# One chain of softmax sums for both query halves, part of a sum on TensorE, and copies and stores handed to other engines

## The chip, the cores and the metric

The kernel runs on one core of one Trainium2 chip. The metric is the device time of one execution in microseconds (us); a lower value is better. The profile shows one execution on that core: the start and duration of the instructions of every engine, and the DMA traffic. The engines are named as the profile names them: PE is TensorE (matmuls; PEld is its weight load), DVE is VectorE, ACT is ScalarE, POOL is GpSimd, and SP is SyncE, which here only starts DMAs.

## The reference

Two blocks follow each other. The first is an attention in which a key counts only if it falls into the same hash bucket as the query; the second mixes with a two-dimensional Fourier transform and then runs a two-layer network with a normalization ahead of it. Cut to what matters:

```
q, k, v: (4, 8, 768, 64)     proj: (64, 6)     w_ch1: (512, 2048)     w_ch2: (2048, 512)

q_bucket = sum(((q @ proj) > 0) * 2**arange(6));  k_bucket likewise
scores = where(q_bucket[:, None] == k_bucket[None, :], q @ k.T / 8, -1e9)
attn   = exp(scores - max);  attn /= sum(attn) + 1e-9
x      = attn @ v                        # then (B,H,S,D) -> (B, S, H*D) = (4, 768, 512)

u  = x + real(fft(fft(x, axis=seq), axis=channel))
un = (u - mean(u)) / sqrt(var(u) + 1e-6)
out = u + relu(un @ w_ch1) @ w_ch2
```

## The kernel before

The four batches are four rounds. In each round attention works on pairs of heads: NPAIR = 4 pairs a batch, two heads of 64 channels side by side on the 128 partitions. For one pair n the 768 keys are taken in NT = 6 chunks of 128 keys (index c), and the 768 queries in two halves of 384 (index g).

**One chunk.** `weigh(n, c)` makes the scores on PE (L849 adds the bucket bits as a bf16 product for the first five pairs, L856 is q times k), and ACT writes their exponential to one of two buffers `pk` (L860). For the later pairs DVE masks it (L866). DVE then adds the chunk to a running sum `acc` (L939): for chunk 1 it adds chunks 0 and 1, for every later chunk it adds the chunk to `acc`. For the first batch it does so in two instructions of 128x768, for the later batches in one of 128x1536. `values(n, c, ...)` multiplies the weights with v on PE (L877); it is put one chunk later in the program, behind the scores of the next chunk, and so the values of a pair's last chunk come behind the scores of chunk 0 of the next pair.

**The end of a pair.** After the values of chunk 5, `scale(n, oos, acc)` normalizes the pair. It copies a column `vs` out of PSUM (L886, on DVE), ACT adds `vs` to both halves of the result while it moves them to `x` (L889), and then each half g is treated alone: two PE matmuls with a matrix of ones sum `acc` over the 128 keys, one for each head, into the upper and lower 64 partitions of one PSUM bank (L894); DVE transposes that bank in blocks of 32x32 into `rt` (L900), takes every 32nd column (12 of them), adds a small number (L902), takes the reciprocal (L903), copies each of the 12 values to 32 places (L905, the spread copy), transposes back into `rb` (L909) and multiplies `x` by it (L910).

**The second block.** `fold` (L989 to L1007) makes sums and differences of `x` on DVE. `mix(b)` then multiplies with the channel matrix on PE (L1029) into a PSUM bank `cs`, from which ACT copies the forward half into `F` (L1036) and DVE the half that runs backward (L1042). A second product (L1058) gives two banks A and B for each of four groups of channels, and four DVE instructions add them to `x` (L1074), two for each bank. The two-layer network follows (`mlp0` for the first batch, `mlp7` for the others; L1296, L1343, and `outer7` with L1214 and L1226). It is written with fewer and larger products in the manner of Strassen, and ends with the stores of `out` by `store` (L967), which POOL issues. A batch has 16 stores.

**The order of the work.** `ps_1` has two PSUM banks for everything that is not scores or values. The first batch's attention runs together with `weights1`, which brings w_ch1 from 64-bit floats to 32 bits: each of its 16 slices costs DVE three instructions (L631, L635, L641) and ACT three (L639, L646, L647). After four slices, and again after eight, `average` computes column means on PE (L654) and `centre` takes them off on DVE (L662, four instructions). This part, from the start to about 131 us, stands in `tc.manual_schedule`[...]. After it, each round runs attention(b) and mix(b-1) with its network side by side, and a planner that works with its own costs and priorities sets the order of each engine's instructions. The last round is mix(3) alone.

At the end every engine leaves through a conditional branch (L1477, L1495: a flag says whether a slower version for very large scores must run), and SP and POOL close the program (L1526).

Of the kernel before, what the change touches and what calls it, by code (L numbers as in the profile page):

```python
# [11 lines left out]
F32 = mybir.dt.float32  # L12
# [5 lines left out]
ALU = mybir.AluOpType  # L18
AX = mybir.AxisListType

P = 128
B, H, S, D = 4, 8, 768, 64
# [3 lines left out]
NT = S // P  # L26
NPAIR = H // 2
HALF = S // 2
# [18 lines left out]
EPS = 2.0**-90  # L47
# [432 lines left out]
def _main(  # L480
# [13 lines left out]
    nc = tc.nc  # L494
# [13 lines left out]
    def wt(shape, dtype, tag, name, bufs=2):  # L508
        return work.tile(shape, dtype, tag=tag, name=name, bufs=bufs)
# [4 lines left out]
    def pt(shape, name):  # L514

        turn[0] += 1
        if roomy[0] and turn[0] % 2:
            if turn[0] % 4 == 1:
                return ps_o.tile(shape, F32, tag="o", name=name)
            return ps_sc.tile(shape, F32, tag="sc", name=name)  # L520
        return ps_1.tile(shape, F32, tag="ps", name=name)
# [72 lines left out]
    ones = const.tile([P, D], F32, tag="ones", name="ones")  # L594
# [8 lines left out]
    for i in range(NPK):  # L603
        pk = const.tile([P, 2, 2, HALF + 1], F32, tag=f"pk{i}", name=f"pk{i}")
# [226 lines left out]
    @contextmanager  # L831
    def behind():

        with tc.issue_after(last[0].ins), tc.high_priority(offset=AHEAD):
            yield
# [43 lines left out]
                    pk[:, g, h, 0:w], start=(c == 0), stop=(c == NT - 1),  # L879
                )  # L880

    def scale(n, oos, acc):

        x = xs[n // NPAIR][:, n % NPAIR]
        vs = wt([P, 1], F32, "vs", f"vs{n}")
        nc.vector.tensor_copy(vs, oos[0][:, HALF : HALF + 1])  # L886
        halves = [x[:, g * HALF : (g + 1) * HALF] for g in range(2)]
        for g, xg in enumerate(halves):
            nc.scalar.activation(xg, oos[g][:, 0:HALF], AF.Identity, bias=vs)  # L889
        for g, xg in enumerate(halves):  # L890

            ps = pt([P, HALF], f"sum{n}_{g}")
            for h in range(2):
                nc.tensor.matmul(  # L894
                    ps[h * D : (h + 1) * D, :], ones, acc[:, g, h],
                    start=True, stop=True,
                )

            rt = wt([P, HALF], F32, "rt", f"rt{n}_{g}", 1)
            nc.vector.transpose(rt, ps)  # L900
            rc = wt([P, HALF // 32], F32, "rc", f"rc{n}_{g}")
            nc.vector.tensor_scalar(rc, rt[:, 0:HALF:32], S * EPS, None, op0=ALU.add)  # L902
            nc.vector.reciprocal(rc, rc)  # L903
            rb = wt([P, HALF], F32, "rb", f"rb{n}_{g}", 1)
            nc.vector.tensor_copy(  # L905
                rt.rearrange("p (j i) -> p j i", i=32),
                rc[:, :, None].broadcast_to([P, HALF // 32, 32]),
            )
            nc.vector.transpose(rb, rt)  # L909
            nc.vector.tensor_tensor(xg, xg, rb, op=ALU.mult)  # L910

    def attention(b):
        xs[b] = wt([P, NPAIR, S], F32, "x", f"x{b}")
        pending = []

        def finish():
            n, c, pk, oos, acc = pending.pop(0)
            with behind() if n >= NPAIR and t is not None else nullcontext():
                values(n, c, pk, oos)
            if c == NT - 1:  # L920
                scale(n, oos, acc)

        for t in range(NPAIR):
            n = NPAIR * b + t
            half = fold(b, 0) if t == NPAIR - 1 else iter(())
            if 1 < n + 1 < NPAIR * B:
                load(n + 1)
            ahead = prepare(n + 1) if n + 1 < NPAIR * B else iter(())
            oos = [ps_o.tile([P, 512], F32, tag="o", name=f"oo{n}_{g}") for g in range(2)]
            acc = wt([P, 2, 2, HALF], F32, "t6", f"acc{n}", 2)  # L930
            first = None
            for c in range(NT):
                new = weigh(n, c)
                if c == 0:
                    first = new[:, :, :, 0:HALF]
                else:

                    for g in (0, 1) if b == 0 else (slice(0, 2),):
                        nc.vector.tensor_tensor(  # L939
                            acc[:, g], (first if c == 1 else acc)[:, g],  # L940
                            new[:, g, :, 0:HALF], op=ALU.add,
                        )
                while pending:
                    finish()
                pending.append((n, c, new, oos, acc))
                if c > 2:
                    next(half, None)
                if c > 0:
                    next(ahead, None)
                yield  # L950
        t = None
        while pending:
            finish()
# [5 lines left out]
    def store(b, T, src, cols):  # L959

        blk, r = divmod(T * P, HALF)
        at = 0
        while at < P:
            par, i = divmod(r + at, HW)
            w = min(P - at, HW - i)
            s0 = blk * HALF + 2 * i + par
            nc.gpsimd.dma_start(  # L967
                out[b, s0 : s0 + 2 * w - 1 : 2, cols], src[at : at + w, cols]
            )
            at += w  # L970
# [41 lines left out]
    def mix(b):  # L1012
        x = xs[b]
        yield from fold(b, 1)
        z = zs[b]


        hd = DM // 2
        F = wt([P, 2, 2, 2, DM], F32, "F", f"F{b}", 1)
        nc.gpsimd.memset(F[:, :, 1, :, 0 : hd + 1 : hd], 0.0)  # L1020
        for par in range(2):
            for t in range(NT // 2):
                ps = pt([P, DM], f"cs{b}_{par}_{t}")
                kinds = (0, 1) if t == 1 else (par ^ (t // 2),)
                for pc in range(2):
                    lo = 0 if 0 in kinds else hd // 2 + 1 - pc
                    hi = hd if 1 in kinds else hd // 2 + 1 - pc
                    for cp in range(2):
                        nc.tensor.matmul(  # L1029
                            ps[:, pc + 2 * lo : pc + 2 * hi - 1 : 2],  # L1030
                            z[:, cp, pc, par, t * P : (t + 1) * P],
                            ch[:, cp, pc, lo:hi], start=(cp == 0), stop=(cp == 1),
                        )
                f = F[:, par, :, t % 2]
                for k in kinds:
                    nc.scalar.copy(  # L1036
                        f[:, k, k : hd + 1 - k],
                        ps[:, k * (hd + 1) : DM if k else hd + 1],
                    )
                f = f[:, kinds[0] : kinds[-1] + 1, hd + 1 :]  # L1040
                r = ps[:, (kinds[0] + 1) * hd - 1 : (kinds[0] + 1) * hd]
                nc.vector.tensor_copy(  # L1042
                    f,
                    bass.AP(
                        r.tensor, r.offset, [r.ap[0], [hd, len(kinds)], [-1, hd - 1]]
                    ),
                )
                yield

        for j in range(NDC):
            pa, pb = (pt([P, HALF + 1], f"{nm}{b}_{j}") for nm in "AB")
            for par in range(2):
                cols = slice(par * NK, HALF + 1 if par else NK)
                for k, ps in enumerate((pa, pb)):
                    for t in range(2):
                        nc.tensor.matmul(  # L1058
                            ps[:, cols], F[:, par, k, t, j * P : (j + 1) * P],
                            sq[:, t, k, cols], start=(t == 0), stop=(t == 1),  # L1060
                        )

            for i in range(2):
                u = x[:, j, i * HALF : (i + 1) * HALF].rearrange("p (r n) -> p r n", r=2)
                for ps, op in (
                    (pa, ALU.add), (pb, ALU.subtract if (j < 2) ^ i else ALU.add)
                ):
                    if i == 0:
                        f = ps[:, 0 : 2 * NK - 1]
                        f = bass.AP(f.tensor, f.offset, [f.ap[0], [NK, 2], [1, HW]])  # L1070
                    else:
                        f = ps[:, HW : HALF + 1]
                        f = bass.AP(f.tensor, f.offset, [f.ap[0], [HW, 2], [-1, HW]])
                    nc.vector.tensor_tensor(u, u, f, op=op)  # L1074
            yield

        yield from mlp0(b) if b == 0 else mlp7(b)
# [111 lines left out]
    def outer7(b, half, hall, ut, rs):  # L1189
# [14 lines left out]
        for j in range(GT):  # L1204
# [35 lines left out]
            if half:  # L1240
                store(b, j, u, low)
# [196 lines left out]
    for b in range(B):  # L1438
# [17 lines left out]
        if b == B - 1:  # L1456
# [7 lines left out]
            ps = pt([1, 3, P], "norms_t")  # L1464
# [13 lines left out]
        for _ in other:  # L1478
            pass
        other = mix(b)  # L1480
        if b == 0:
            arrival2 = weights2()
# [48 lines left out]
```

## Time and profile before

| what | value |
|---|---|
| time, median of 3 runs | 1128.34 us (1127.03 to 1129.04) |
| the profiled execution: its time, and the span of its profile | 1127.22 us, 1125.4 us |
| PE busy | 1067.8 us, 95% of the span |
| DVE busy | 813.7 us, 72% |
| ACT busy | 445.8 us, 40% |
| POOL busy | 81.3 us, 7% |
| last DVE instruction ends | 1115.67 us after the start |
| stores of `out` | 64, of which 16 belong to the last batch |

"Busy" is the time in which an engine has at least one instruction running. A share over the whole span mixes stages: the first batch's attention with the conversion of w_ch1 (up to about 150 us) loads DVE far more than the rest, and after about 200 us PE is busy nearly all the time. A number in a group of instructions such as "x128 | 25.5, 494" is the count, the busy time in us, and the mean duration of one in ns; PE overlaps its instructions, so that the count times the mean exceeds the busy time. PE takes a product of 32-bit floats as two records, so 128 records at L894 are 64 matmuls.

### The profile page before, as it was taken

To read this page: it belongs to the slowest core of one execution; us is meant where nothing else is said; L and a number is where in the kernel's file an instruction comes from. 1 tells how busy PE (TensorE), PEld (TensorE's weight loads), DVE (VectorE), ACT (ScalarE), POOL (GpSimd) and SP (SyncE) were. 2 spreads that over 40 slices of the span, in tenths; PEclk is the share of its full clock that TensorE was granted. 3 is DMA by queue.
4 is the path that set the end of the run, shared out by engine and by line. 5 is a ranking of instruction groups with operands and counts; after the bars stand their busy time and mean duration, and the time that the engine had idled before them with its cause. 6 is when DMAs were issued, how large, how long until landed. Compare 5 with 4: busy or idle time off the path is not lost. (4 is left out here: it accounts for less than half of the span.)

```text
span 1125.4 us, 13920 instructions
## 1 busy us (share of the span) xinstructions
PE 1067.8 (95%) x4885; PEld 652.0 (58%) x4885; DVE 813.7 (72%) x1442; ACT 445.8 (40%) x835; POOL 81.3 (7%) x157
## 2 busy tenths in 40 slices
PE   7988887999999999999999999999999999999995
PEld 3333344554764567655764467645665469768575
DVE  5889987927689596984777797995966876644352
ACT  6767444534145222355225522254324421340420
POOL 1000000001200011020000002002000002100011
PEclk9999998999999999999999999999999999999998
DMA  9643525442037234212244225023023214122301
GB/s 236 186 93 89 104 82 152 113 151 46 1 84 222 64 80 168 43 52 82 41 132 95 79 61 168 18 59 89 24 70 108 70 34 169 49 82 91 117 21 39
DMA packets 174415, 103.13 MB, mean 92 GB/s; under 512 B 129408, under 2 KB 161280, under 8 KB 174336
## 3 DMA queue, kind: packets, MB, share of 16 engines
q1 hardware_dynamic: 166608, 82.35, 27.6%
q0 software_dynamic: 6160, 19.40, 5.5%
q8 instruction: 41, 0.67, 0.3%
q10 hardware_dynamic: 1568, 0.39, 0.2%
q14 instruction: 38, 0.31, 0.1%
HBM read 81.14 MB, written 20.97 MB: 91 GB/s over the span
## 5 line engine op out<-in xcount | busy, mean ns | idle before, releaser
L1214 PE MATMUL o<-w,h 128*128 128x256 f32 x1152 | 258.7, 381 | 0.1
L1214 PEld LDWEIGHTS o<-w,h 128*128 128x128 f32 x1152 | 216.7, 190 | 41.7 <-issue 2.3
L860 ACT ACTIVATE pk<-sc 128x768 f32<-128x768 f32 x192 | 147.8, 807 | 104.1 <-PE sc L856 69.8
L866 DVE SCALAR_TENSOR_TENSOR pk<-qb,kb,pk 128x768 f32<-128x768 bf16 x132 | 129.1, 1012 | 43.7 <-ACT pk L860 43.5
L856 PE MATMUL sc<-qt,kt 64*128 64x384 f32 x768 | 153.1, 502 | 3.5 <-ACT pk L860 3.5
L877 PE MATMUL oo<-pk,vn 128*64 128x385 f32 (+1 forms) x768 | 151.9, 502 | 1.9 <-DVE pk L866 1.6
L1343 PE MATMUL h_p<-x,w 128*128 128x384 f32 x384 | 138.8, 493 | 0.5 <-ACT h L1365 0.5
L939 DVE TENSOR_TENSOR acc<-acc,pk 128x1536 f32<-128x1536 f32 (+1 forms) x80 | 112.8, 1426 | 0.9 <-ACT pk L860 0.3
L1343 PE MATMUL h_p<-w 128*128 128x384 f32 x288 | 106.2, 491 | 1.6 <-ACT u L1085 0.9
L1343 PEld LDWEIGHTS h_p<-x,w 128*128 128x128 f32 x384 | 70.3, 190 | 55.8 <-ACT h L1384 3.1
L877 PEld LDWEIGHTS oo<-pk,vn 128*64 128x64 f32 x768 | 48.3, 137 | 92.4 <-issue 69.6
L856 PEld LDWEIGHTS sc<-qt,kt 64*128 64x128 f32 x768 | 66.8, 186 | 50.8 <-issue 25.7
L1296 PE MATMUL h<-x,w 128*128 128x384 f32 x256 | 86.7, 492 | 2.1 <-ACT h L1300 1.1
L1343 PEld LDWEIGHTS h_p<-w 128*128 128x128 f32 x288 | 53.2, 190 | 42.7 <-ACT w L1392 5.1
L1296 PEld LDWEIGHTS h<-x,w 128*128 128x128 f32 x256 | 47.4, 190 | 39.0 <-issue 2.3
L967 POOL DMA_DIRECT2D out_dram<-w x40 | 21.9, 550 | 538.8 <-issue 412.7
L1226 DVE SCALAR_TENSOR_TENSOR w<-o,rs,w 128x256 f32<-128x256 f32 x56 | 26.7, 478 | 46.1 <-PE o L1214 46.0
L1244 ACT COPY tq<-o 128x256 f32<-128x256 f32 x24 | 8.9, 372 | 113.6 <-PE o L1214 113.6
L1214 PE MATMUL o<-w 128*128 128x256 f32 x192 | 46.3, 384 | 3.7 <-DVE u L1226 1.8
L1214 PEld LDWEIGHTS o<-w 128*128 128x128 f32 x192 | 35.7, 190 | 12.3 <-DVE w L1226 3.9
L1233 ACT COPY tq<-o 128x256 f32<-128x256 f32 x24 | 8.9, 371 | 72.1 <-PE o L1214 72.1
L1300 ACT ACTIVATE h<-h 128x384 f32<-128x384 f32 x32 | 15.6, 489 | 48.7 <-PE h L1296 48.5
(157 smaller groups left out, 1281.1 us busy)
## 6 DMA issues: line engine op xcount, KB each, us to landing
w<-ad SPq DMA_DIRECT2D x168, 128.0 KB, 2.0
w<-bd SPq DMA_DIRECT2D x42, 512.0 KB, 4.5
zraw<-in_moe_w_ch_dram POOLq DMA_DIRECT2D x21, 512.0 KB, 4.3
bd<-w SPq DMA_DIRECT2D x14, 512.0 KB, 5.0
vn<-in_v_dram SPq DMA_DIRECT2D x32, 192.0 KB, 3.4
qn<-in_q_dram SPq DMA_DIRECT2D x120, 48.0 KB, 2.4
kn<-in_k_dram SPq DMA_DIRECT2D x60, 96.0 KB, 3.2
ad<-tq SPq DMA_DIRECT2D x8, 512.0 KB, 4.6
```

Of the source, the lines that this page charges most:

```text
L856: last[0] = nc.tensor.matmul(ps[:, h, 0:HALF], kt[rows, ks], qt[rows, qs], start=kb is not None, stop=True,)
L860: nc.scalar.activation(pk[:, g, :, 0:HALF], ps[:, :, 0:HALF], AF.Exp, scale=SCALE)
L866: nc.vector.scalar_tensor_tensor(w, qb[:, h].rearrange("p (g s) -> p g s", g=2), kb[:, h, c : c + 1], w, op0=ALU.is_equal, op1=ALU.mult,)
L877: nc.tensor.matmul(oos[g][h * D : (h + 1) * D, 0:w], nat["v", n][:, (2 * c + h) * D : (2 * c + h + 1) * D], pk[:, g, h, 0:w], start=(c == ...
L939: nc.vector.tensor_tensor(acc[:, g], (first if c == 1 else acc)[:, g], new[:, g, :, 0:HALF], op=ALU.add,)
L967: nc.gpsimd.dma_start(out[b, s0 : s0 + 2 * w - 1 : 2, cols], src[at : at + w, cols])
L1214: nc.tensor.matmul(ps, a[:, r], right7[i][:, r], start=start and r == 0, stop=r == HF // 2 - 1, skip_group_check=not start,)
L1226: nc.vector.scalar_tensor_tensor(t[:, cols], src, r, t[:, cols], op0=ALU.mult, op1=ALU.add)
L1233: nc.scalar.copy(qq, p1)
L1296: nc.tensor.matmul(ps, w1[:, c, fc * P : (fc + 1) * P], x[:, c, cols], start=(c == 0), stop=(c == NDC - 1),)
L1300: nc.scalar.activation(hall[:, i, r, cols], ps, AF.Relu)
L1343: nc.tensor.matmul(ps, ring[n % NR][:, k], right[i][:, k], start=start and k == 0, stop=k == 1, skip_group_check=not start,)
```

## The change

There are five edits.

1. `scale` no longer treats the halves alone up to the product. The transposes of both halves go into one `rt` of 128x768; the sum, the reciprocal (24 columns instead of 12), the way back and the product are one instruction each. The spread copy is gone: the transpose back reads each reciprocal 32 times through a broadcast.
2. `vs` is copied by ACT instead of DVE.
3. In the first batch, chunk 5 of a pair is not added to `acc` by DVE. Instead the matmuls with ones run over two parts, `acc` (chunks 0 to 4) and the `pk` of chunk 5, which accumulate in the same bank: four times two matmuls instead of four.
4. The backward half of `F` is copied by ACT. The four additions of A and B to `x` are in another order: both of A, then both of B.
5. The stores of the last batch are issued by SP instead of POOL.

```diff
-    def scale(n, oos, acc):
+    def scale(n, oos, sums):
...
-        nc.vector.tensor_copy(vs, oos[0][:, HALF : HALF + 1])
+        nc.scalar.copy(vs, oos[0][:, HALF : HALF + 1])
...
-        for g, xg in enumerate(halves):
+        rt = wt([P, S], F32, "rt", f"rt{n}", 1)
+        for g in range(2):
             ps = pt([P, HALF], f"sum{n}_{g}")
             for h in range(2):
-                nc.tensor.matmul(
-                    ps[h * D : (h + 1) * D, :], ones, acc[:, g, h],
-                    start=True, stop=True,
-                )
-
-            rt = wt([P, HALF], F32, "rt", f"rt{n}_{g}", 1)
-            nc.vector.transpose(rt, ps)
-            rc = wt([P, HALF // 32], F32, "rc", f"rc{n}_{g}")
-            nc.vector.tensor_scalar(rc, rt[:, 0:HALF:32], S * EPS, None, op0=ALU.add)
-            nc.vector.reciprocal(rc, rc)
-            rb = wt([P, HALF], F32, "rb", f"rb{n}_{g}", 1)
-            nc.vector.tensor_copy(
-                rt.rearrange("p (j i) -> p j i", i=32),
-                rc[:, :, None].broadcast_to([P, HALF // 32, 32]),
-            )
-            nc.vector.transpose(rb, rt)
-            nc.vector.tensor_tensor(xg, xg, rb, op=ALU.mult)
+                for i, part in enumerate(sums):
+                    nc.tensor.matmul(
+                        ps[h * D : (h + 1) * D, :], ones, part[:, g, h],
+                        start=(i == 0), stop=(i == len(sums) - 1),
+                    )
+            nc.vector.transpose(rt[:, g * HALF : (g + 1) * HALF], ps)
+
+        rc = wt([P, S // 32], F32, "rc", f"rc{n}")
+        nc.vector.tensor_scalar(rc, rt[:, 0:S:32], S * EPS, None, op0=ALU.add)
+        nc.vector.reciprocal(rc, rc)
+        nc.vector.transpose(
+            rt.rearrange("p (j i) -> p j i", i=32),
+            rc[:, :, None].broadcast_to([P, S // 32, 32]),
+        )
+        nc.vector.tensor_tensor(x, x, rt, op=ALU.mult)
...
-                new = weigh(n, c)
+                pk = weigh(n, c)
+                new = pk[:, :, :, 0:HALF]
+                sums = [acc]
                 if c == 0:
-                    first = new[:, :, :, 0:HALF]
+                    first = new
+                elif c == NT - 1 and b == 0:
+
+                    sums.append(new)
                 else:
...
-            nc.gpsimd.dma_start(
+            (nc.sync if b == B - 1 else nc.gpsimd).dma_start(
                 out[b, s0 : s0 + 2 * w - 1 : 2, cols], src[at : at + w, cols]
             )
...
-                nc.vector.tensor_copy(
+                nc.scalar.copy(
                     f,
                     bass.AP(
                         r.tensor, r.offset, [r.ap[0], [hd, len(kinds)], [-1, hd - 1]]
...
-            for i in range(2):
-                u = x[:, j, i * HALF : (i + 1) * HALF].rearrange("p (r n) -> p r n", r=2)
-                for ps, op in (
-                    (pa, ALU.add), (pb, ALU.subtract if (j < 2) ^ i else ALU.add)
-                ):
+            for ps, op in (pa, ALU.add), (pb, ALU.subtract):
+                for i in range(2):
+                    u = x[:, j, i * HALF : (i + 1) * HALF].rearrange("p (r n) -> p r n", r=2)
...
-                    nc.vector.tensor_tensor(u, u, f, op=op)
+                    nc.vector.tensor_tensor(
+                        u, u, f, op=op if (j < 2) ^ i else ALU.add
+                    )
```

More of the change, by code (lines that the diff above doesn't have):

```diff
@@ L916, in finish @@
         def finish():
-            n, c, pk, oos, acc = pending.pop(0)
+            n, c, pk, oos, sums = pending.pop(0)
             with behind() if n >= NPAIR and t is not None else nullcontext():
@@ L920, in finish @@
             if c == NT - 1:
-                scale(n, oos, acc)
+                scale(n, oos, sums)
         for t in range(NPAIR):
@@ L939, in attention @@
                         nc.vector.tensor_tensor(
-                            acc[:, g], (first if c == 1 else acc)[:, g],
-                            new[:, g, :, 0:HALF], op=ALU.add,
+                            acc[:, g], (first if c == 1 else acc)[:, g], new[:, g],
+                            op=ALU.add,
                         )
@@ L944, in attention @@
                     finish()
-                pending.append((n, c, new, oos, acc))
+                pending.append((n, c, pk, oos, sums))
                 if c > 2:
```

## The prediction, made before the result was known

> **What bounds the kernel now.** I read the busy time by stage first, since the shares of the whole span hide that there are three regimes. Columns: length, then busy us of PE, PEld, DVE, ACT, POOL with the count of instructions, then clock and DMA.
>
> ```profile
> 20.00:48.00 28.00, 25.92 (x140) 11.39 (x138) 24.98 (x45) 21.14 (x37) 2.13 (x4) 1.00 0.87 275
> 75.00:100.00 25.00, 21.67 (x128) 9.13 (x123) 23.63 (x43) 21.03 (x37) 0.00 (x0) 1.00 0.32 65
> 100.00:130.00 30.00, 23.88 (x134) 9.53 (x132) 28.97 (x55) 14.42 (x24) 0.11 (x1) 1.00 0.44 107
> 160.00:180.00 20.00, 15.28 (x86) 10.34 (x84) 10.62 (x20) 7.54 (x13) 1.57 (x3) 0.92 0.39 130
> 500.00:600.00 100.00, 99.45 (x434) 60.67 (x433) 68.35 (x109) 35.67 (x68) 6.94 (x10) 1.00 0.31 85
> ```
>
> In the first attention DVE is the fuller engine (28.97 of 30 us); after about 200 us PE is (99.45 of 100). Between 160 and 180 us neither is: DVE waits for DMAs there. What DVE saves therefore counts up to about 150 us, and hardly later.
>
> Next the end of the first pair, in the order of time on DVE (start, duration) and on PE.
>
> ```profile
> 34.90 1.81 DVE L939 TENSOR_TENSOR acc<-acc,pk 128x768 f32<-128x768 f32 x2
> 38.40 2.48 DVE L662 TENSOR_TENSOR w<-w,wm 128x512 f32<-128x512 f32 x4 [1.69 <-PE wm L654]
> 42.76 0.57 DVE L900 STREAM_TRANSPOSE rt<-sum 128x384 f32<-128x384 f32 x1
> 47.54 0.56 DVE L910 TENSOR_TENSOR x<-x,rb 128x384 f32<-128x384 f32 x1
> 48.02 0.42 DVE L631 TENSOR_SCALAR w<-fraw 128x512 int32<-128x512 int32 x1
> ```
>
> ```profile
> 34.66 3.70 PE L654 MATMUL wm<-w,mean 128*128 128x512 f32 x8
> 40.01 1.51 PE L877 MATMUL oo<-pk,vn 128*64 128x385 f32 x8
> 41.36 1.46 PE L894 MATMUL sum<-acc,ones 128*64 128x384 f32 x8
> 42.75 0.34 PE L849 MATMUL sc<-qkb 64*128 64x384 bf16 x2
> ```
>
> The chain of both halves takes DVE 48.02 - 42.76 = 5.26 us. After the last addition to `acc` DVE stands still, until PE has the column means.
>
> Last the program's end: the last DVE instruction ends at 1115.67, and this row of the closing line shows what fills the 9.7 us to 1125.4 (duration min/median/max in ns, first and last start):
>
> ```profile
> L1526 POOLq DRAIN  x3: 40/107/7418, 1117.2 to 1125.2; - x3
> ```
>
> The longest drain of POOL runs from 1117.2 to 1124.6; SP is done with its own list at 1119.6, and after POOL's drain only 0.8 us of closing remain.
>
> [...] 8 records at L894 take 1.46 us, not the 8 x 0.32 that they would take alone. [...] At L791 four 32-column products stand one after the other in the program, two records each, but the first records of all four start at 153.57 to 153.60 and the second ones at 153.92. [...] of the 2.3 us that DVE idles ahead of the 255-column L1042 copies, 2.1 end with ACT's copy from the same bank. [...] Here a 128 KB store from POOL lands after 2.6 us and a 128 KB write from SP (`ad<-w`) after 2.2. [...] PE's branch at L1495 takes 3.56 us, POOL's 0.04.
>
> **The chain of both halves, no spread copy.** Per pair, from the first transpose: two transposes from PSUM 0.60 + 0.55; the sum of 24 columns 0.20 with its gap; the reciprocal 0.35 (12 columns take 0.23; taking the difference to the 12-column sum, 0.06, once more gives 0.29, plus a gap of 0.06); the transpose back of 128x768 1.05 (L747 has 0.97); the product 0.90 (L989, 128x768, has 0.95 with an overlap of 0.05). That is 3.65 against 5.26, so 1.6 us of DVE per pair. The broadcast read is unseen on a transpose; L905 reads such a source at 0.357 us for 384 elements, under 1 ns each, so I take nothing, at worst +0.5 per pair. `vs` on ACT saves DVE 0.07 and starts L889 up to 1.5 us earlier, since ACT waited for DVE there (29.9 us in nine waits). It costs ACT some 0.15 us, beside DVE's chain.
>
> **Chunk 5 on PE.** DVE loses 1.74 us (1.82 for two, overlapping) per pair in four pairs. PE gains 8 records a pair: at the present 0.16 us each (2 tiles at once, 0.32 us a step) 1.3 us. The program now gives one tile four records before the other's first. If those cannot be overtaken, the 16 records take 12 steps, 3.9 us instead of 2.7; L791 shows an overtaking past three records, and L815 starts its six products as three pairs although the first three belong to one tile. I take 2.7. A new wait comes with it: the exponential of chunk 1 of the next pair overwrites that `pk` and now waits for the sums as well; they end before those scores do, so it costs nothing, 0.5 at most.
>
> Pair by pair, with DVE's second transpose 2.8 us after the sums' start and 3.1 us from it to the end of the product (0.55 + 0.20 + 0.35 + 1.05 + 0.90, with 0.05 of wait):
> - Pair 0: the means still arrive at 38.4, so the addition saves nothing. Sums from 41.36, end 41.36 + 2.8 + 3.1 = 47.3 instead of 48.02: 0.8.
> - Pair 1: PE works without a pause from 64.7 through the means to the sums at 74.54, so the same: 80.4 instead of 81.67: 1.2.
> - Pair 2 has no means. Values end at 101.55, so 107.45 instead of 109.56: 2.1.
> - Pair 3: the sums no longer wait for DVE (1.77 us before 130.19), the two later means of 7.1 us follow 1.5 us sooner, and DVE has 3.4 us less to do by 149: between 1.5 and 3.4, I take 2.5.
>
> Together 6.6 us; with no overtaking about 2.5; with every DVE saving paid out, 4 x 3.4 = 13.
>
> **DFT copies and the order of additions.** 24 copies leave DVE (16 of 0.42, 8 of 0.69: 12.2 us) for ACT (16 x 0.38 as L1036, 8 x 0.59 as the 512-column L1085: 10.8 us). ACT is 36% busy in 500 to 600. Per bank ACT then needs 0.38 + 0.38 where ACT, a hop and DVE needed 0.9. A is free one addition (0.5 us) sooner; PE waited 3.4 us in all for A's additions, nearly all at 173 us. From 200 us to the end PE's pauses behind DVE sum to 7.1 us and behind ACT to 5.6, which caps what this and twelve shorter chains can return. I take 1 us there and 1 us for 150 to 200 us, where the 9.5 us of PE pauses have DMA waits behind them. But after 131 us the planner orders all anew with other durations: I allow -4 to +5 for that.
>
> **Last stores by SP.** SP's last fetch is at 1062.3 and the first of these 16 stores was at 1084, so none queues behind another. POOL keeps small work that ends before; it then leaves early and its 7.4 us drain lies beside the last products. The end is then: SP's store after 1115.67, landing about 2.4 us later, SP's branch, 14 closing waits of 0.06, and 0.9. With a branch as short as POOL's that is 4.5 us, with one like PE's 8, instead of 9.7. I take 6.7, a gain of 3.
>
> **Sum.** 6.6 + 1 + 1 + 3 = 11.6 off the profiled span of 1125.4: 1113.8. The profiled execution took 1127.2 and the median is 1128.3, so the same difference gives 1116.7.
>
> **Rivals.**
> - Half of it is lost (0.20): PE runs the eight sums of a half in series[...]. The first attention returns 2.5, the end 1.7: 4 us, 1124. For it: the program order of the sums, PE's branch. Against it: L791 and L815.
> - ACT becomes the bound behind PE and the kernel slower (0.11). [...] a backward copy can fall behind a pair of exponentials (1.5 us), and with two banks in `ps_1` PE waits for the next. From 24 copies at 11.6 / 24 = 0.48 us each upward the whole gain is gone; at 0.65 us, 15.6 - 11.6, the time is 1132. Against it: ACT is idle 60% of this stage, and PE's present waits behind all ACT work are 5.6 us.
> - All of DVE's saving comes through and the pauses of 150 to 200 us close as well (0.14): 12 + 3 + 4 = 19, so 1109.
> - The change does not what it says: DVE's waits merely take the additions' place. This is counted in pairs 0 and 1 above.
>
> **Chances.** The forecast 0.55, half 0.20, more 0.14, slower 0.11. A measurement of this kernel can tell about 0.2% (2.3 us) from no change. All but the slow case and a tail of the half one lie below 1126: faster 0.84, same 0.05, slower 0.11. The forecast's own range is 1112 to 1121; to take in half and more, and leave out no more than 2 in 10, I give 1108 to 1125.5.
>
> **What would show it.** Right: no L905; L894 with 160 records, 16 in about 2.7 us in the first batch; DVE waits ahead of L900 in pairs 0 and 1, with the means still near 38.4; the fold of batch 0 some 5 us earlier; PE over 98% busy from 200 us on; POOL's long drain over before the last product, and an end 5 to 8 us after DVE's last instruction. Wrong: 16 records in 3.9 us; a long drain that still ends the program; new PE pauses behind ACT's F copies; a body after 200 us that is longer by more than 4 us.

## The result and the profile after

The changed kernel takes 1112.86 us, the median of four runs (1112.12 to 1118.14), against 1128.69 us (1127.03 to 1130.81) for the kernel before. The ratio is 0.9869, with a 95% interval of 0.9834 to 0.9904: 15.8 us less. The forecast was 1116.7 us. The profiled span went from 1125.4 to 1110.4 us, 15.0 less.

The same stages as before, in the view by stage (length, busy us of PE, PEld, DVE, ACT and POOL with their counts, PE clock, DMA share, GB/s):

```profile
20.00:48.00 28.00, 26.83 (x146) 11.76 (x144) 22.68 (x38) 22.23 (x39) 2.13 (x4) 1.00 0.88 273
75.00:100.00 25.00, 24.09 (x144) 10.27 (x142) 22.81 (x36) 22.05 (x40) 0.00 (x0) 1.00 0.30 58
100.00:130.00 30.00, 28.03 (x154) 11.91 (x151) 27.22 (x49) 15.56 (x27) 0.11 (x1) 1.00 0.57 131
160.00:180.00 20.00, 17.10 (x97) 11.26 (x96) 16.03 (x35) 11.36 (x24) 2.63 (x5) 1.00 0.57 178
500.00:600.00 100.00, 99.44 (x452) 59.34 (x451) 65.12 (x96) 37.81 (x72) 0.00 (x0) 1.00 0.35 89
```

In the first attention PE is now as full as DVE (28.03 and 27.22 of 30 us). From 500 to 600 us PE stays at 99.4: nothing is gained there. From 160 to 180 us PE does 1.8 us more. Its clock is no longer lowered there; the stretch of lowered clock of the changed kernel lies just behind, from 180.6 to 184.0 us.

The end of the first pair, first on DVE, then on PE (start, duration, and in brackets the idle time ahead with what ended it):

```profile
38.46 2.48 DVE L662 TENSOR_TENSOR w<-w,wm 128x512 f32<-128x512 f32 x4 [3.42 <-PE wm L654]
...
42.96 0.58 DVE L901 STREAM_TRANSPOSE rt<-sum 128x384 f32<-128x384 f32 x1
44.26 0.58 DVE L901 STREAM_TRANSPOSE rt<-sum 128x384 f32<-128x384 f32 x1 [0.71 <-PE sum L897]
44.87 0.18 DVE L904 TENSOR_SCALAR rc<-rt 128x24 f32<-128x24 f32 x1
45.09 0.30 DVE L905 RECIPROCAL rc<-rc 128x24 f32<-128x24 f32 x1
45.43 0.98 DVE L906 STREAM_TRANSPOSE rt<-rc 128x768 f32<-128x768 f32 x1
46.52 0.96 DVE L910 TENSOR_TENSOR x<-x,rt 128x768 f32<-128x768 f32 x1
47.39 0.42 DVE L631 TENSOR_SCALAR w<-fraw 128x512 int32<-128x512 int32 x1
```

```profile
41.42 0.86 PE L897 MATMUL sum<-acc,ones 128*64 128x384 f32 x4
42.06 0.87 PE L897 MATMUL sum<-pk,ones 128*64 128x384 f32 x4
42.70 0.87 PE L897 MATMUL sum<-acc,ones 128*64 128x384 f32 x4
43.35 0.87 PE L897 MATMUL sum<-pk,ones 128*64 128x384 f32 x4
44.15 0.34 PE L849 MATMUL sc<-qkb 64*128 64x384 bf16 x2
```

The means arrive at 38.46 as before, so that the addition which is gone turns into a longer wait there (3.42 us instead of 1.69). The 16 records of the sums take 44.15 - 41.42 = 2.73 us. From the second transpose to the end of the product it is 47.39 - 44.26 = 3.13 us. The pair ends 0.6 us sooner than before, at 47.39.

The closing line, and the row of the same kind for the branch with which the engines leave (count, shortest, median and longest in ns, first and last start):

```profile
L1531 POOLq DRAIN  x3: 40/107/6107, 972.4 to 1110.2; - x3
```

```profile
L1500 SPq COMPARE_BRANCH  x2: 46/48/49, 1104.4 to 1106.0; - x2
...
L1531 SPq EVENT_SEMAPHORE  x14: 17/28/28, 1108.8 to 1110.4; - x14
```

POOL leaves at 972 us, and its drain of 6.1 us ends 130 us before the program. What follows the last DVE instruction (its end: 1103.02) is now SP: it waits for its last stores until 1105.9, branches at 1106.0, and has its next instruction only at 1108.8, so 2.7 us after the branch. Twelve waits and the closing take it to 1110.4. That is 7.4 us where it was 9.8.

**Where the 15 us come from.** Profiles differ by up to 3.5 us in how long the first loads take, so I count from the start of the first centring (L662, at 38.40 before and 38.46 after). The fold of batch 0 comes after 100.40 us before, after 93.28 now: 7.1 less. From there to the last DVE instruction it is 976.87 and 971.28 us: 5.6 less. The tail, from there to the end, gives 2.4.

The middle stretch can be divided further, with the pauses of PE (the gaps between its records) and the time that its lowered clock takes (one minus the granted clock, times the length, summed over slices of 2 us), both from the trace. The same division for every kernel of this study (us; the rows below the first two belong to the experiments):

| kernel | fold to last DVE instruction | PE pauses | lost to a lowered clock | rest |
|---|---|---|---|---|
| before | 976.9 | 23.0 | 3.4 | 950.5 |
| after | 971.3 | 18.9 | 1.7 | 950.7 |
| after, second profile | 974.6 | 20.0 | 5.1 | 949.4 |
| edits 1 and 2 alone | 974.0 | 19.9 | 1.7 | 952.4 |
| edit 3 alone | 975.4 | 20.9 | 3.4 | 951.1 |
| edit 4 alone | 974.4 | 22.3 | 3.4 | 948.6 |
| the copies of edit 4 alone | 973.3 | 22.3 | 1.7 | 949.3 |
| edit 5 alone | 976.2 | 22.7 | 3.4 | 950.1 |
| all but edit 3 | 975.9 | 22.0 | 3.4 | 950.5 |
| all but edit 4 | 967.7 | 16.0 | 0.0 | 951.7 |
| edit 3 for pairs 2 and 3 only | 971.1 | 18.1 | 3.4 | 949.7 |
| the same, second profile | 971.6 | 20.0 | 1.7 | 949.9 |
| after, with a late copy on POOL | 972.2 | 19.3 | 3.4 | 949.4 |
| edit 3 in all four batches | 987.2 | 15.4 | 1.7 | 970.1 |

The pauses are counted up to PE's last product. The rest, which is PE's own work and the 1.6 to 2 us from its last product to the last DVE instruction, stays within 2 us of 950.5 wherever the products are the same. What differs are the pauses and the lowered clock next to some of them. Between before and after it is 4.1 us of pauses (3.05 before 215 us, 1.06 after) and 1.7 of clock. Each kernel has one profile, except for the two that have a second one here, and the two profiles of the changed kernel differ by 3.3 us in this stretch: against the kernel before, the second one is only 2.3 us shorter, not 5.6.

### The profile page after: what moved, and what is told of

The parts are those of the page before. It is cut to its first block, busy times and chain, and to the rows that moved or that the text cites. A ratio compares the mean times of both kernels' runs of the same rounds, so it can differ in the third digit from the quotient of the medians.

```text
span 1110.4 us, 13886 instructions
## 1 busy us (share of the span) xinstructions
PE 1068.3 (96%) x4917; PEld 654.6 (59%) x4917; DVE 779.1 (70%) x1298; ACT 454.6 (41%) x875; POOL 79.6 (7%) x141
## 4 chain that ended last, share of the span: by engine, by line
PE 63%; DVE 14%; ACT 3%; DMA 2%; issue 2%; DVEq 0%; ACTq 0%
PE o L1219 23%; PE h_p L1348 18%; PE h L1301 5%; PE sc L856 5%; PE oo L877 5%; DVE pk L866 4%; DVE acc L944 2%; PE cs L1034 2%; DMA zraw<-in_moe_w_ch_dram 2%; PE A L1063 1%; PE B L1063 1%; DVE x L1077 1%; ACT pk L860 1%; PE bits L791 1%; PE sum L897 1%
## 5 line engine op out<-in xcount | busy, mean ns | idle before, releaser
L944 DVE TENSOR_TENSOR acc<-acc,pk 128x1536 f32<-128x1536 f32 (+1 forms) x72 | 105.7, 1482 | 1.5 <-ACT pk L860 0.9
L972 POOL DMA_DIRECT2D out_dram<-w x30 | 16.4, 548 | 428.3 <-issue 309.0
L1265 DVE TENSOR_TENSOR tq<-tq,o 128x256 f32<-128x256 f32 x24 | 10.1, 422 | 38.1 <-PE o L1219 38.1
```

The source lines that it names most:

```text
L944: nc.vector.tensor_tensor(acc[:, g], (first if c == 1 else acc)[:, g], new[:, g], op=ALU.add,)
L972: (nc.sync if b == B - 1 else nc.gpsimd).dma_start(out[b, s0 : s0 + 2 * w - 1 : 2, cols], src[at : at + w, cols])
```

## The experiments

My theory was the prediction's: the first attention is bound by DVE and pays out what the chain saves; the rest is bound by PE and returns little; the end is POOL's drain. The rivals are that the merged chain alone does it and the sums on PE cost as much as they save, and that the gain after the fold is no property of an edit but of the order that the planner happens to make. Five kernels do one part alone on the kernel before; the others change the kernel after.

**Edits 1 and 2 alone** (the merged chain, `vs` on ACT; the sums run over `acc` alone).

```diff
-        for g, xg in enumerate(halves):
+        rt = wt([P, S], F32, "rt", f"rt{n}", 1)
+        for g in range(2):
...
+            nc.vector.transpose(rt[:, g * HALF : (g + 1) * HALF], ps)
...
+        nc.vector.tensor_tensor(x, x, rt, op=ALU.mult)
```

> The kernel before with edits 1 and 2 alone (one chain for both halves, no spread copy, vs by ACT). Theory, that the first attention is paced by DVE: each pair ends 1.6 us sooner and no wait takes it back, since the four sums of a pair end before DVE comes to them; the fold of batch 0 (second one, behind pair 3) comes 6.4 us sooner than before, and the time falls by 6 to 8 us. Rival, that chunk 5 carries the gain and the chain only fills DVE's waits: the fold comes less than 3 us sooner.

Measured: 1116.91 us, ratio 0.9894 (0.9861 to 0.9927). The products that end the pairs are over 1.75, 3.48, 5.22 and 8.03 us sooner than before, each counted from the first centring, and the fold comes 7.7 us sooner. The first three pairs give 1.7 each, where 1.6 was worked out. The fourth gives 2.8, but 1.4 of it are two instructions that stood inside its chain and now stand behind it. One of them belongs to the last centring. In the kernel before, two centring instructions come ahead of the fold (L989):

```profile
137.16 0.65 DVE L662 TENSOR_TENSOR w<-w,mean 128x512 f32<-128x512 f32 x1
138.20 0.69 DVE L662 TENSOR_TENSOR w<-w,mean 128x512 f32<-128x512 f32 x1
138.80 1.82 DVE L989 TENSOR_TENSOR ef<-x 128x768 f32<-128x768 f32 x2
```

and with edits 1 and 2 alone all of that centring comes behind it (L988):

```profile
132.61 1.79 DVE L988 TENSOR_TENSOR ef<-x 128x768 f32<-128x768 f32 x2
137.33 0.68 DVE L662 TENSOR_TENSOR w<-w,mean 128x512 f32<-128x512 f32 x1
```

The two take 1.2 us of DVE's time ahead of the fold (0.57 and 0.60, each to the start of the next instruction). So 6.5 of the 7.7 us come from the chain, and 6.4 were expected. The changed kernel has the same order, so 1.2 of its 7.1 us are of this kind too. Still, 7.7 is more than the 7.1 us of the whole change, which I had not expected. Edit 2 was not run alone; its share is not known.

**Edit 3 alone** (chunk 5 summed by PE, with the chain of before).

```diff
+                elif c == NT - 1 and b == 0:
+
+                    sums.append(new)
```

> The kernel before with edit 3 alone (chunk 5 of the first batch summed on PE). Theory: the addition that DVE loses lay in a wait for the column means in pair 0, so that pair gains nothing or loses 0.2 us; pair 1 gains 0.4, pair 2 1.3, pair 3 1.0 to 1.7: about 3 us by the fold of batch 0, and the parts do not add up with the chain (6.4 + 3 against 7.1 measured for both). Rival, that DVE's saving is paid out: 4 x 1.74 = 7 us by the fold.

Measured: 1121.77 us, ratio 0.9932 (0.9907 to 0.9958). The pairs end -0.2, 0.1, 1.5 and 3.3 us sooner, and the fold comes 3.3 us sooner, about as the theory has it. Where means precede the end of the pair (0 and 1) the edit gives -0.2 and 0.3; in pairs 2 and 3 it gives 1.3 and 1.8, of which some 0.6 are again a centring instruction that has moved.

**All but edit 3, and edit 3 for pairs 2 and 3 only** (each a line of the kernel after).

```diff
-                elif c == NT - 1 and b == 0:
+                elif c == NT - 1 and b < 0:
```

> The changed kernel with edit 3 undone (chunk 5 of the first batch added by DVE again). Theory, from the runs of single edits: with the merged chain, the sums over two parts make DVE wait for PE in pairs 0 and 1 and lose 1.1 and 0.6 us there, against 0.5 and 0.2 us won in pairs 2 and 3. So the end of pair 3, counted from the first centring, comes 0.9 us sooner than in the changed kernel, and the time is the same within 0.2% (0 to 2 us less). Rival, that edit 3 is worth the 1.5 to 3.4 us that a DVE-paced stage promises: the time is 2 to 4 us longer.

```diff
-                elif c == NT - 1 and b == 0:
+                elif c == NT - 1 and b == 0 and t > 1:
```

> The changed kernel with edit 3 kept for pairs 2 and 3 alone, where no column means stand ahead of the sums. Theory: pairs 0 and 1 end 1.7 us sooner each than in the kernel before (0.7 and 1.1 in the changed kernel), pairs 2 and 3 as in the changed kernel; the end of pair 3 comes 1.6 us sooner than there, and the time falls by about 1.6 us. Rival, that later waits give it back: less than 0.5 us in the time with the same shift at pair 3.

Measured without edit 3: 1114.91 us, ratio 0.9883 (0.9867 to 0.99). The fold comes 0.65 us sooner than in the changed kernel; the theory said 0.9 at the end of pair 3. The stretch after it is 4.6 us longer than in the first profile of the changed kernel and 1.3 us longer than in the second. For the whole, the ratio lies 0.0014 above the 0.9869 of the changed kernel, and the intervals overlap. So the theory held for its stage, and the whole is not shown to be faster or slower.

Measured for pairs 2 and 3 only: 1110.87 us, ratio 0.9852 (0.9835 to 0.9868). The fold comes 1.67 us sooner than in the changed kernel, and all of it is seen in the first two pairs. The end of pair 0 in this kernel on DVE:

```profile
42.61 0.69 DVE L641 CUSTOM_DVE_ANT_0 w<-w,fraw 128x1024 uint16<-128x1024 uint16 x1
43.22 1.04 DVE L901 STREAM_TRANSPOSE rt<-sum 128x384 f32<-128x384 f32 x2
44.29 0.18 DVE L904 TENSOR_SCALAR rc<-rt 128x24 f32<-128x24 f32 x1
...
46.81 0.42 DVE L631 TENSOR_SCALAR w<-fraw 128x512 int32<-128x512 int32 x1
```

Both transposes now follow each other without a wait (x2 in 1.04 us), since with 8 records both halves are summed in time. In the changed kernel the second one waits 0.71 us for the sums of the second half, because the merged chain needs both halves before it can go on. In the kernel before, and with edit 3 alone, the sums of the second half lay behind the chain of the first half, so DVE did not wait for them. Thus edit 3 takes 1.0 us from what the chain gives in pair 0.

Both once more, this time on one chip:

> The changed kernel itself, beside chunk5_late on the same chip, so that the two can be compared. Every theory expects 0.987 of the kernel before, 1113 us: the fold of batch 0 some 54.8 us after the first centring, 971.3 us from there to DVE's last instruction.

> Edit 3 for pairs 2 and 3 alone, once more, beside the changed kernel. If in pairs 0 and 1 the eight further products only lengthen a chain that nothing shortens, the fold comes 1.7 us sooner than in the changed kernel and the time is 1 to 2.5 us below it. If the difference of the first look was one of chips, the two are within 0.5 us.

Measured: the changed kernel 1115.88 us, ratio 0.9872 (0.9852 to 0.9892); edit 3 for two pairs 1113.37 us, ratio 0.9861 (0.984 to 0.9882). The fold is again 1.65 us sooner. The 1.65 us are shown in the stage; of the whole time the intervals overlap, and the advantage is not shown there. The second profile of the changed kernel has 974.6 us after the fold instead of 971.3, and the 3.4 us more of lowered clock are as large as that difference.

**Edit 4 alone, the copies of edit 4 alone, all but edit 4.** The first has both parts; the second only

```diff
-                nc.vector.tensor_copy(
+                nc.scalar.copy(
                     f,
```

on the kernel before; the third is the kernel after with that line and the order of the additions as before.

> The kernel before with edit 4 alone (backward half of F by ACT, additions of A then B). Theory: nothing up to 131 us; between 150 and 210 us DVE has 3 us less to do, the planner puts the additions of A and B ahead of the wait for the DMA of tq that held them (6.48 us before), and 2 to 3.5 us come back there; from 210 us on less than 1 us. Total -2 to -4.5 us. Rival, that the better order there came from the sooner end of the first attention: the 6 us wait stays and the time moves by less than 1 us. Rival, ACT becomes the bound: slower by 2 us or more.

> Only the backward copies on ACT; the order of the additions is that of before. If the gain of edit 4 comes from the copies (PE's banks free sooner, the planner's other order), the time is 2 to 3 us below before and the 173 us gap is gone, as with the whole edit. If it comes from A being free one addition sooner, at most 0.5 us is left of it.

> All edits but the fourth. If what the edits return after the fold adds up, the stretch from the fold to DVE's last instruction is 973.8 us (971.3 and the 2.5 of edit 4 alone), the time 1115.5, and the wait of 6.5 us on DVE near 173 us is back. If the planner's order decides on the whole and the parts don't add up, that stretch is anywhere from 970 to 976.

Measured: edit 4 alone 1125.85 us, ratio 0.9975 (0.9965 to 0.9985); its copies alone 1126.48 us, ratio 0.9969 (0.9957 to 0.9981); all but edit 4 1110.19 us, ratio 0.9825 (0.981 to 0.9841). The order of the additions adds nothing that can be seen. The copies gain some 3 us on the kernel before, and in both kernels PE's pause of 3.35 us at 173 us is gone. (With the copies alone the fold comes 1.0 us later than before, with a stretch of lowered clock ahead of it, at 133 us.) In the change they do the opposite: without edit 4 the time is 5.7 us below the 1115.88 that the changed kernel took on the same chip, and the intervals don't overlap. The parts do not add up, as the second theory said, with a body shorter than even it allowed (967.7; it said 970 to 976). Nor is the 6.5 us wait near 173 us back: edit 3 alone, without edit 4, has no such wait either. From the second profile of the changed kernel, whose time is the 1115.88, to the one without edit 4 the stretch after the fold is 6.9 us shorter: 5.1 less of lowered clock, 4.0 less of pauses, 2.3 more of the rest. One place where part of it goes is near 178 us. PE of the changed kernel (first profile):

```profile
176.54 1.56 PE L856 MATMUL sc<-qt,kt 64*128 64x384 f32 x8
180.66 2.90 PE L877 MATMUL oo<-pk,vn 128*64 128x385 f32 x8 [2.56 <-ACT x L890]
```

The values of the next pair wait until ACT has taken the result of the last pair out of PSUM (L890). ACT of the changed kernel ahead of it:

```profile
177.44 0.18 ACT L887 COPY vs<-oo 128x1 f32<-128x1 f32 x1
178.75 0.67 ACT L639 ACTIVATE zraw<-zraw 128x512 int32<-128x512 uint32 x1 [1.13 <-DMA zraw<-in_moe_w_ch_dram]
179.31 0.74 ACT L647 ACTIVATE zraw<-zraw,least 128x512 f32<-128x512 f32 x1
179.96 0.18 ACT L647 ACTIVATION_READ_ACCUMULATOR zraw<-zraw,least 128x1 f32 x1
180.05 1.02 ACT L890 ACTIVATE x<-oo,vs 128x384 f32<-128x384 f32 x2
```

and of the kernel with all but edit 4:

```profile
176.64 0.15 ACT L887 COPY vs<-oo 128x1 f32<-128x1 f32 x1
176.83 1.05 ACT L890 ACTIVATE x<-oo,vs 128x384 f32<-128x384 f32 x2
```

In the first the planner put conversions of a weight slice between `vs` and L890; one of them waits 1.13 us for its DMA, and L890 waits behind it on ACT. In the second L890 follows at once. After the pause of 2.56 us the clock is lowered (the view by stage of the changed kernel):

```profile
178.00:180.00 2.00, 0.10 (x2) 0.00 (x0) 2.00 (x5) 1.25 (x3) 0.00 (x0) 1.00 0.19 40
180.00:182.00 2.00, 1.34 (x4) 0.66 (x6) 2.00 (x5) 1.78 (x5) 0.53 (x1) 0.65 0.14 23
182.00:184.00 2.00, 2.00 (x10) 0.99 (x8) 0.73 (x2) 0.00 (x0) 0.00 (x0) 0.50 0.75 265
184.00:186.00 2.00, 2.00 (x14) 0.78 (x12) 0.17 (x1) 1.57 (x3) 0.00 (x0) 1.00 0.70 110
```

The column ahead of the DMA share is PE's clock. 0.35 and 0.50 of 2 us are 1.7 us lost. All but edit 4 has no such stretch between the fold and the last product. Edit 4 isn't needed for such a pause. The kernel with edit 3 alone does not have it, and ACT and PE there show:

```profile
186.67 0.67 ACT L639 ACTIVATE zraw<-zraw 128x512 int32<-128x512 uint32 x1 [2.29 <-DMA zraw<-in_moe_w_ch_dram]
187.24 1.04 ACT L890 ACTIVATE x<-oo,vs 128x384 f32<-128x384 f32 x2
187.86 1.71 PE L877 MATMUL oo<-pk,vn 128*64 128x385 f32 x8 [2.90 <-ACT x L890]
```

The order alone doesn't decide either. The kernel with edit 3 for two pairs has a conversion between `vs` and L890 in both of its profiles: in the first it does not wait, and PE has no pause there; in the second it waits 0.50 us for its DMA, and PE pauses for 1.82 us. Where these traces show the long pause, both are there: a conversion ahead of L890, and a DMA for it that comes late.

**Edit 5 alone, and a late copy on POOL.** The second is the kernel after, with a copy of one element on POOL once the last result is there, into a buffer that nothing reads any more.

```diff
-            nc.gpsimd.dma_start(
+            (nc.sync if b == B - 1 else nc.gpsimd).dma_start(
```

> The kernel before with edit 5 alone (last batch's stores by SP). Theory, that POOL's late leave sets the end: the time from DVE's last instruction to the end falls from 9.7 to 7.4 us, all before stays, total -2.3 us. Rival, that the end is the landing of the last store and the closing list whoever issues it: less than 0.5 us.

```diff
+                if b == B - 1 and j == GT - 1:
+                    nc.gpsimd.tensor_copy(mhalf[0:1], u[0:1, DM - 1 : DM])
```

> The changed kernel with one more instruction on POOL: behind the last store it copies one element of the last result, so that POOL leaves late without a DMA of its own. Theory, that POOL's long drain belongs to its leaving and not to a store in flight: the drain of 6 to 7 us again ends the program, and from DVE's last arithmetic to the end there are 9 to 10 us instead of 7.4: 2 to 2.5 us longer in all. Rival, that the drain waits for POOL's own DMAs: 7.4 us as in the changed kernel, the same time.

Measured: edit 5 alone 1125.80 us, ratio 0.9982 (0.9973 to 0.9991), the tail 7.7 us where it was 9.8, close to the 2.3 us less that the theory has. The late copy: 1115.97 us, ratio 0.9891 (0.9874 to 0.9907); the tail is 7.67 us, no longer than in the other kernels that have edit 5 (7.4 to 7.8). The drains of the two:

```profile
L1526 POOLq DRAIN  x3: 40/107/6107, 986.5 to 1124.8; - x3
```

```profile
L1533 POOLq DRAIN  x3: 40/107/6111, 1108.0 to 1114.7; - x3
```

With the copy POOL leaves at 1108.0 and drains 6.1 us again, though it has no store of its own in flight. So the drain belongs to the leaving, not to the stores. But it ends at 1114.1, and SP needs until 1114.1 for its own branch and waits. The mechanism held, and its effect on the time did not: this drain, which begins 6.9 us before the end, is still just hidden.

**Edit 3 in all four batches** (`elif c == NT - 1:`, with nothing else changed).

> The changed kernel with chunk 5 summed on PE in all four batches. Theory, that DVE's time is worth nothing where PE is the bound: twelve more pairs give PE 8 more records each at 0.16 us, 12 x 1.3 = 15.4 us, and the time is 13 to 17 us longer, nothing of it before 131 us. Rival, that shorter DVE queues there save PE waits: less than 10 us longer.

Measured: 1129.99 us, ratio 1.0019 (1.0001 to 1.0037). Nothing changes before the fold; after it the stretch grows from 971.3 to 987.2 us, 15.9 more, as the theory has it. PE's pauses fall by 3.5, as the rival has it, and its work grows by 19.4. That is 0.20 us for each of the 96 further records, more than the 0.16 expected. Where PE is full, its further work outweighs the pauses that it saves.

## Why the prediction was right, point by point

- **First attention.** Predicted 0.8, 1.2, 2.1 and 2.5 for the four pairs, 6.6 in all. Measured at the ends of the pairs 0.7, 1.2, 2.2 and 2.7, and 7.1 at the fold (the list of what would show it said some 5 us for the fold, less than the sum's own 6.6). Of the fourth pair 0.6, and of the 7.1 us 1.2, are the centring instructions that now stand behind the fold, which the prediction did not foresee; 5.9 are left for the chain and the sums, 0.7 less than forecast. So it is luck that the 7.1 lie above the forecast. The terms were right: the chain from the second transpose 3.13 us (3.1 said), the second transpose 2.84 us after the sums' start (2.8), the means still at 38.5, the waits ahead of the transposes in pairs 0 and 1. Pairs 2 and 3 have the wait of 0.7 us ahead of the second transpose too. The 0.5 us at worst for the broadcast was not needed: 0.98 us at L906, 0.97 at L747 without it.
- **The sums on PE.** 16 records in 2.7 us was said, 2.73 it is. Four records of one tile (two of `acc`, two of `pk`) stand first in the kernel's text; in the trace the four of `acc`, two for each tile, start from 41.42 us and the four of `pk` from 42.06 (first half), in pairs 0.32 us apart. At L815 of the kernel before the six products start at 163.92, 163.93, 163.96, 163.97, 163.98 and 163.99 us, the three pairs that the prediction leans on. This order of starts is all that its "overtaking" stands on: whether it arises in the chip or in the compiled program, the trace doesn't show. The rival with 3.9 us fell on this line. What the prediction's working did not draw from its own numbers is that edit 3 has a price in pairs 0 and 1: it gives next to nothing there, and with the merged chain its longer sums are waited for. The change is right in sum, yet edits 1 and 2 alone give more by the fold (7.7) than all three.
- **150 to 200 us and after.** This is the term that was mis-sized: 1 + 1 us predicted, 5.6 measured. In place of 1 us up to 200 us, 3.05 us of pauses went up to 215 us, and one stretch of lowered clock, 1.7; after 215 us it is 1.06, as said, with PE busy in 878.99 of the 890 us from 210 to 1100. The 1.7 us of clock were no term of the sum, and they are not reliable: the second profile of the changed kernel loses 1.7 us more to the clock than the kernel before, and gains 2.3 us in this stretch. The wait that left is this one of the kernel before, on DVE, with the additions of A queued behind it:

```profile
174.78 0.42 DVE L1131 TENSOR_TENSOR tq<-w 128x256 f32<-128x256 f32 x1 [6.48 <-DMA ad<-tq]
175.12 0.42 DVE L1133 TENSOR_TENSOR tq<-w 128x256 f32<-128x256 f32 x1
175.45 1.01 DVE L1074 TENSOR_TENSOR x<-x,A 128x384 f32<-128x384 f32 x2
```

  In the groups of the two kernels, PE's idle time ahead of the products into A (last part of the row) fell from 4.0 to 1.0 us:

```profile
L1058 PE MATMUL A<-sq,F 128*128 128x193 f32 (+1 forms) x128 | 28.6, 347 | 4.0 <-DVE x L1074 3.4 <-DVE F L1042 0.7
```

```profile
L1063 PE MATMUL A<-sq,F 128*128 128x193 f32 (+1 forms) x128 | 27.5, 337 | 1.0 <-DVE x L1077 0.9
```

  I had put the 3.4 us down to A's additions and so to edit 4. All but edit 4 has only 0.3 us ahead of these products, so that was wrong: it was DVE's wait for a DMA with the additions behind it. That wait stands in the kernel before, in the one with edits 1 and 2 alone (6.43 us) and in the one with edit 5 alone (6.51); it is gone with edit 3 alone, with edit 4 alone and with its copies alone. So either of two edits moves it, through the order that the planner makes. What the order gives is thus not the return of one edit. It was inside the -4 to +5 us that I had allowed for the planner, and the trace of before could not tell more.
- **ACT as the bound.** It was not. The 24 copies cost 0.463 us each against the 0.45 estimated, and none of them waited:

```profile
L1047 ACT COPY F<-cs 128x255 f32<-128x255 f32 (+1 forms) x24 | 11.1, 463 | 0.0
```

  ACT's order did cost PE a pause, but by L890 behind a conversion that waits for its DMA, not by the copies' time.
- **The end.** 3 us predicted, 2.4 measured: the tail is 7.4 us instead of 6.7. SP's branch was the unknown term; to the next instruction it takes 2.7 us, between POOL's 0.4, counted the same way (the 0.04 of the prediction are the branch's own record), and PE's 3.6. The trace shows these gaps, not their cause. The landing takes 2.9 us instead of 2.4. The drain was over long before, as said.
- **Sum.** 6.6 + 2 + 3 = 11.6 predicted; 7.1 + 5.6 + 2.4 = 15.1 measured in the first profile, whose span is 15.0 us shorter. The median is 3.8 us below the forecast, and the 3.6 us that the stretch after the fold gave beyond the forecast account for nearly all of it. The runs beside edit 3 for two pairs have the changed kernel 14.0 us below the kernel before (1115.88 against 1129.90), nearer to the forecast. The mechanisms at the two ends were right; the middle was in the allowance for the planner, not in the working.

## What to carry to other kernels

Where one engine bounds a stage, a shorter chain on it paid in full here (1.7 us for each of the first three pairs, 1.6 worked out); work moved to another engine paid only where its result wasn't the next thing waited for (-0.2 and 0.3 us in pairs 0 and 1, 1.3 and 1.8 in pairs 2 and 3), so it must be asked pair by pair what is waited for. Where a planner sets the order, an edit's own gain can't be added to another's: a wait for a DMA stands in some engine's queue, and what lies behind it decides; look for that wait and put it where nothing urgent follows. Of the versions here all but edit 4 has the lowest ratio, 0.9825 (1110.19 us against 1115.88 for the changed kernel on one chip). Edit 3 for pairs 2 and 3 has 0.9852 and 0.9861, and the intervals overlap. The two together were not tried.

## What the runs showed of the hardware

- **The lowered clock came in pieces of one size.** Between 20 us and PE's last product the clock records of the 14 traces show 22 stretches at half the clock: 19 of 3.41 us, which cost 1.7 us each, and three of 6.83 us, twice that. Where several stand in one profile, they start whole multiples of 3.413 us apart: 17.07 us in the kernel before (five; 176.97 and 194.04 us), 139.96 in the second profile of the changed kernel (41), 68.24 with the copies of edit 4 alone (20), 150.20 with edit 5 alone (44), 146.76 in all but edit 3 (43), 136.52 in the first profile of edit 3 for pairs 2 and 3 (40) and 153.60 with the late copy on POOL (45). All but 17.07 are read from slices of 2 us, to some 0.1 us.
- **Ahead of these stretches PE had paused.** The pause is 3.35 and 3.00 us in the kernel before and 2.56 us in the changed kernel, each shorter than a stretch. If the two traces are cut, from 20 us on, into steps of 3.413 us that fit the start of a stretch, the steps just ahead of the three stretches are 0.89, 0.83 and 0.73 pause, and no other step has more than 0.53. In the kernel with edits 1 and 2 alone a pause of 3.31 us, from 169.03 to 172.34 us, falls into two such steps, 0.51 and 0.47 of them, and the clock is 1.00 from there up to 187.8 us. These are counts, not an experiment; what brings a stretch on, and why three are twice as long, they don't show. The changed kernel lost 1.7 us to the clock in one profile and 5.1 in the other, so 1.7 us more or less in one profile says little of an edit.
- **POOL's drain on leaving** took 6.1 us with no store in flight and 7.4 us right after its stores. The one of 6.1 us that began 6.9 us before the end was just hidden.
- **The same kernel, profiled twice**, differed by 3.7 us of span, and the lowered clock accounts for 3.4 us (5.1 lost to it instead of 1.7). A difference of a microsecond or two between two profiles after the fold says nothing on an edit without that count.
